# Order and queues of the first transfers, the products ahead of the data, and the place of one q fetch, in a linear-attention and gated-MLP kernel

## The chip, the cores and the metric

The kernel runs on one core of one Trainium2 chip. The metric is device microseconds of one execution. A core has five engines with instruction queues of their own: PE (TensorE, matrix products), DVE (VectorE), ACT (ScalarE), POOL (GpSimd) and SP (SyncE, which here only issues transfers). Each engine works its instructions off in program order and waits where an operand is not ready. Sixteen DMA engines move the data; transfers are issued from SP, ACT or POOL.

## The reference

The inputs are q, k and v with shape (8, 8, 576, 64): batches, heads, tokens and head size, in fp32. The weights w_in (512 x 2048) and w_out (2048 x 512) come in 64-bit floating point.

```python
kv  = einsum('bhsd,bhse->bhde', k, v)          # 64 x 64 per head
o   = einsum('bhsd,bhde->bhse', q, kv)
rms = sqrt(mean(o * o, axis=-1) + 1e-6)
x   = (o / rms * g_norm)                       # heads side by side: (4608, 512)
h   = x @ w_in
sp  = maximum(h, 0) + log1p(exp(-abs(h)))      # softplus
out = (h * erf(sp)) @ w_out                    # (4608, 512)
```

## The kernel before

**Tiling.** The 4608 tokens are worked off in nine groups of 512 (G): T = 0 to 7 are the first 512 tokens of each batch, T = 8 the last 64 tokens of all eight batches together. In a group the heads go in four pairs (p = 0 to 3), since two heads of 64 fill the 128 partitions. After attention a group has xT, four blocks of 128 x 512. The hidden layer goes in 16 parts of 128 columns (f = 0 to 15): four products of 128x512 for h, softplus and erf on ACT, the gate h * erf(sp) on DVE, and four products into the output sums, which are made LAG = 5 parts later.

**Groups.** Groups 0 and 1 use plain fp32 products. In the page, one plain fp32 product of 128x512 is two records of L971 or L674. From group 2 on, weights and activations are cut into parts of a shorter format (L618). The 64-bit weights are turned into fp32 while group 0 runs: a raw piece is loaded (load_w, L243), split into exponent and mantissa words on ACT (w_split, L267: L274 and L275) and joined with integer operations on DVE (w_join, L278: L285 to L298). There are RAW = 4 buffers for raw pieces, so a later load waits for a join. The order of pieces is w_order (L301): the parts f = 0 to 3 of w_in alone, then f = 4 and 5 together, two parts of w_out, and so on.

**The front.** Nothing can overlap ahead of group 0, so its attention is written out by hand in ORDER (L61 to L68). Every name there is a small function; name and pair make one step. For a pair p of group 0: kv (the products of k and v, L724), kv_out (DVE copies the two 64x64 blocks, L735), q (four transposes on PE, L741), q_out (ACT copies the result, L745), result (one product, L748), square (ACT, L751), mean (one product with a constant matrix, L755), log, root and again (ACT, L759, L762, L765), and norm_a, norm_b and norm_c (DVE, L768, L773, L780), after which xT of the pair is there. split is one w_split. join is join_load (L823): one w_join, the next raw load and two of the transfers kept in the list to_fetch. tail stands for the 64 last tokens. next0 and next1 call load_pair for pairs 4 and 5, which are the first two pairs of group 1 ("the fifth pair" is pair 4).

**Transfers.** load_pair (L138) issues k, v and q of one pair of group 0: 288 KB, 288 KB and 256 KB. The queues alternate: `sides` is ACT, SP, ACT, ... for pairs 0 and 2 and begins with SP for pair 1; pair 3 is SP alone. So k0, q0, v1, k2 and q2 go from ACT, and v0, k1, q1, v2, k3, v3 and q3 from SP. For group 1 and later, k and v of a pair are issued at once or put in to_fetch, and load_q (L180) puts eight transfers for q into to_fetch, 32 rows with runs of 128 bytes each, because this q is transposed later on DVE in 32x32 blocks (turn, L349, at L353). fetch_some(n) (L198) issues the next n of to_fetch on SP. In group 0 it runs in each join (two), and at the end of each part n (four, L1024). POOL issues the four transfers of q_last and two of g_col.

**Ahead of the data.** DVE fills mean_f and eps_col and casts mean_f to mean_w (L214 to L218). Then PE runs WARM = 24 products of mean_w with itself, 128x128 each (L828 to L830), whose result nobody reads. After them come the first four raw loads (RAW, L831), then ORDER.

**After the front.** The loop over n (L918) runs the 16 parts of group 0 and of group 1. For n = 0, 1 and 2 the products are interleaved by block of xT (L964 to L967); from n = 3 on a part has its four products in a row. At the start of part n = 4 come the products for the kv of pair 4 (prepare, L388) and on DVE kv_kept and turn(1, 0) (keep_prepared, L397); after that part comes the first product of pair 4 with its transposed q (visit, L426, at L433).

Of the kernel before, what the change touches and what calls it, by code (L numbers as in the profile page):

```python
# [39 lines left out]
FP32 = mybir.dt.float32  # L40
FP32R = mybir.dt.float32r
I32 = mybir.dt.int32
# [14 lines left out]
WHOLE = 2  # L57
SHIFT = 4096.0
SQ = 32
WARM = 24  # L60
ORDER = """  # L61
kv0 q0 q_out0 kv_out0 result0 kv1 q1 square0 mean0 kv_out1 q_out1 log0 result1
kv2 kv_out2 root0 square1 q2 again0 q_out2 mean1 norm_a0 tail norm_b0 log1 tail_out
kv3 q3 root1 again1 q_out3 split norm_c0 kv_out3 tail_result result2 result3 square2 split mean2
next0 square3 norm_a1 split mean3 log2 root2 norm_b1 tail_kept again2
join log3 root3 join next1 again3 softplus norm_c1 join norm_a2 split norm_b2 norm_c2 norm_a3
norm_b3 norm_c3 split join
"""  # L68


# [1 line left out]
def kernel(  # L72
# [10 lines left out]
    nc = tc.nc  # L83
    P = 128
# [3 lines left out]
    G = J * P  # L88
# [18 lines left out]
    early = early_room.enter_context(tc.tile_pool(name="early", bufs=2))  # L107
# [21 lines left out]
    def chunks(T):  # L129

        return 6 if T == 0 else 5

    def rows_in(T, c):

        rows = S // chunks(T) // 16 * 16
        return rows + (S - chunks(T) * rows if c == 0 else 0)

    def load_pair(i, later=False):  # L138
        T, p = divmod(i, NP)
        if T >= B:  # L140
            return
        pool = early if i in (2, 3) else kvp
        sides = [nc.scalar, nc.sync] * 3 if i < 3 else [nc.sync] * 6
        sides = sides[i % 2 :]
        for name, got, src in (("k", k_sb, k), ("v", v_sb, v)):
            side = sides.pop(0)
            C = chunks(T)
            rows, rest = rows_in(T, 1), rows_in(T, 0) - rows_in(T, 1)
            t = got[T, p] = pool.tile([rows + rest, 2, C, D], FP32, name=f"{name}_sb", tag=name)
            heads = src[T, 2 * p : 2 * p + 2]  # L150
            due_ = [
                partial(
                    side.dma_start,
                    out=t[:rows].rearrange("r h c d -> r h (c d)"),
                    in_=heads[:, : S - rest].rearrange("h (r c) d -> r h (c d)", c=C),
                )
            ]
            if rest:
                due_.append(
                    partial(  # L160
                        side.dma_start,
                        out=t[rows:, :, 0],
                        in_=heads[:, S - rest :].rearrange("h r d -> r h d"),
                    )
                )
            if later:
                to_fetch.extend(due_)
            else:
                for start in due_:
                    start()  # L170
        if T > 0:
            load_q(i)
            return
        t = pool.tile([P, G if pool is early else S], FP32, name="q_sb", tag="q")
        t = q_sb[T, p] = t[:, 0:G].rearrange("p (j h d) -> p j h d", j=J, h=2)
        sides.pop(0).dma_start(
            out=t, in_=q[T, 2 * p : 2 * p + 2, 0:G, :].rearrange("h (p j) d -> p j h d", j=J)
        )

    def load_q(i):  # L180


        T, p = divmod(i, NP)
        t = q_sb[T, p] = kvp.tile([P, S], FP32, name="q_sb", tag="q")
        for n in range(P // SQ):
            h, w = divmod(n, D // SQ)
            to = t[n * SQ : n * SQ + SQ].rearrange("a (j b) -> a j b", b=SQ)
            for head, js in ((1 - h, slice(0, G // 2 // SQ)), (h, slice(G // 2 // SQ, S // SQ))):
                src = q[T, 2 * p + head, :, w * SQ : w * SQ + SQ]
                to_fetch.append(  # L190
                    partial(
                        nc.sync.dma_start,
                        out=to[:, js],
                        in_=src.rearrange("(j a) b -> a j b", a=SQ)[:, js],
                    )
                )

    def fetch_some(n):  # L198
        for due_ in to_fetch[:n]:
            due_()  # L200
        del to_fetch[:n]

    for i in range(NP):
        load_pair(i)
# [6 lines left out]
    eps_col = const.tile([P, 1], FP32, name="eps_col")  # L211
    mean_w = const.tile([P, P], FP32R, name="mean_w")
    mean_f = early.tile([P, 2 * G], I32, name="mean_f", tag="w_e", bufs=2).bitcast(FP32)[:, 0:P]
    nc.vector.memset(mean_f, 0.0)  # L214
    for i in range(2):
        nc.vector.memset(mean_f[i * D : i * D + D, i * D : i * D + D], 1.0 / D)
# [92 lines left out]
    def w_next(what):  # L309
        i = w_at[what]  # L310
        if i < len(w_order):
            w_at[what] = i + 1
            {"load": load_w, "split": w_split, "join": w_join}[what](*w_order[i][1:])
# [87 lines left out]
    def attention(T, p, in_parts=False):  # L401
# [136 lines left out]
        def loads():  # L538
            load_pair(T * NP + p + 2, later=True)
# [283 lines left out]
    def join_load():  # L823
        w_next("join")
        w_next("load")
        fetch_some(2)

    warm = ps_h.tile([P, G], FP32, name="warm_ps", tag="h")  # L828
    for _ in range(WARM):
        nc.tensor.matmul(warm[:, 0:P], lhsT=mean_w, rhs=mean_w, start=True, stop=True)  # L830
    for _ in range(RAW):  # L831
        w_next("load")
    do = {
# [4 lines left out]
        "split": partial(w_next, "split"),  # L838
        "softplus": softplus_table,
        "join": join_load,  # L840
        "next0": partial(load_pair, NP),
        "next1": partial(load_pair, NP + 1),
    }
    for p in range(NP):
        do |= first_group(p)
# [72 lines left out]
    for n in range(FIRST * FC + 1):  # L918
# [39 lines left out]
        elif T < FIRST:  # L958
# [11 lines left out]
            for i, c in blocks:  # L970
                nc.tensor.matmul(  # L971
                    plain[i],
                    lhsT=w_in_sb[:, i % FC, c],
                    rhs=xT[T][:, c, :],
                    start=(c == 0),
                    stop=(c == KC - 1),
# [97 lines left out]
    for m in range(first_batch, batches + 1):  # L1074
# [3 lines left out]
        if T + 1 < NG:  # L1078
            todo = list(attention(T + 1, b, in_parts=last_))
            if b == 0:  # L1080
                side = late_r if T % 2 == FIRST % 2 else late
# [30 lines left out]
        if m < batches:  # L1112

            pool, tag = (acc, "e") if m % 2 else (wide, "b")
# [102 lines left out]
```

## Time and profile before

| what | us |
|---|---|
| median of 3 runs | 911.84 |
| lowest and highest run | 910.84, 913.04 |
| the profiled execution's time | 912.09 |
| its span in the profile | 910.3 |
| warm-up products (L830), start and length | 1.68, 5.38 |
| first products of k and v (L724), start | 6.99 |
| first h product (L971), start | 25.93 |
| first product with q of the fifth pair (L433), start | 45.51 |

The span is the time between the first and the last instruction that the profiler saw; 1.8 us of the profiled execution lie outside it. Rows of the timeline give the start and the length in us, the engine, the line of the kernel, the operation, "written tile <- read tiles", the shape and how often; in brackets stands how long the engine had been idle and what ended the idle time. PE is a row of products and PEld the loads of their weights; SPq, ACTq and POOLq are the times in which an engine issued a transfer.

### The profile page before, as it was taken

The page shows a single profiled execution, that of the slowest core. Times are in us where ns is not written, and L with a number is a line of the kernel's source. Part 1 is how long each engine was busy: PE and PEld are TensorE (multiplying, and loading weights), DVE is VectorE, ACT ScalarE, POOL GpSimd, SP SyncE. Part 2 cuts the span into 40 slices and gives each one's busy share as a digit, 9 for nine tenths or more (in the row PEclk, how much of TensorE's full clock was granted, in tenths as well). Part 3 has the DMA queues.
Part 4 walks back from the last instruction along what each step waited for, and adds up shares of the span by engine and source line. Part 5 has one row for each costly group of instructions (what it writes and reads, how often), then busy time and mean ns, then how long its engine had stood idle before and what let it go on. Part 6 is the DMA issues. An engine that isn't in the chain of part 4 may idle for free.

```text
span 910.3 us, 13631 instructions
## 1 busy us (share of the span) xinstructions
PE 901.2 (99%) x5014; PEld 673.4 (74%) x5014; DVE 749.3 (82%) x1084; ACT 593.5 (65%) x784; POOL 4.7 (1%) x14
## 2 busy tenths in 40 slices
PE   8999999999999999999999999999999999999998
PEld 6344445666678888888888888888888888888886
DVE  2799958997688888888888888888888888887777
ACT  4977666776766667667666666666666666665552
POOL 2000000000000000000000000000000000000000
PEclk9999999999999999999999999999999999999999
DMA  9877507999699998999799989999897787778871
GB/s 273 237 244 220 156 0 259 356 365 357 191 337 357 352 323 274 328 348 328 260 327 349 312 277 306 341 326 310 277 354 266 268 319 302 286 285 319 319 263 49
DMA packets 145506, 259.91 MB, mean 286 GB/s; under 512 B 81504, under 2 KB 104032, under 8 KB 145440
## 3 DMA queue, kind: packets, MB, share of 16 engines
q1 hardware_dynamic: 142144, 256.98, 82.6%
q10 hardware_dynamic: 3104, 1.93, 0.8%
q8 instruction: 40, 0.66, 0.3%
q14 instruction: 26, 0.21, 0.1%
q0 software_dynamic: 192, 0.13, 0.1%
HBM read 224.40 MB, written 34.60 MB: 285 GB/s over the span
## 4 chain that ended last, share of the span: by engine, by line
PE 94%; DMA 3%; ACT 1%; DVE 1%; issue 0%; SPq 0%; DVEq 0%
PE n_ps L618 48%; PE m_ps L618 24%; PE o_ps L674 10%; PE h_ps L971 5%; PE at_ps L447 2%; PE at_ps L433 2%; DMA w_out_parts<-w_out 1%; DMA v_sb<-in_v_dram 1%; DMA q_sb<-in_q_dram 1%; PE at_ps L485 1%; PE at_ps L486 1%; DMA w_raw<-in_moe_w_in_dram 1%; PE warm_ps L830 1%; PE kv_ps L724 0%; PE o_ps L748 0%
## 5 line engine op out<-in xcount | busy, mean ns | idle before, releaser
L618 PE MATMUL n_ps<-w_out_parts,g_forms 128*128 128x512 f32 x928 | 230.7, 390 | 0.8 <-DMA w_out_parts<-w_out 0.8
L618 PE MATMUL n_ps<-x_forms,w_in_parts 128*128 128x512 f32 x896 | 224.3, 392 | 0.0
L618 PEld LDWEIGHTS n_ps<-w_out_parts,g_forms 128*128 128x128 f32 x928 | 172.6, 188 | 36.9 <-DMA w_out_parts<-w_out 1.6
L618 PEld LDWEIGHTS n_ps<-x_forms,w_in_parts 128*128 128x128 f32 x896 | 166.6, 188 | 35.7 <-ACT s_sb L916 0.2
L596 DVE TENSOR_TENSOR h<-m_ps,h 128x512 f32<-128x512 f32 x116 | 78.2, 687 | 69.1 <-PE m_ps L618 65.5
L618 PE MATMUL m_ps<-w_out_parts,g_forms 128*128 128x512 f32 (+1 forms) x468 | 124.3, 388 | 0.0
L618 PE MATMUL m_ps<-x_forms,w_in_parts 128*128 128x512 f32 x448 | 119.7, 389 | 0.0
L1123 ACT ACTIVATE h<-n_ps 128x512 f32<-128x512 f32 x112 | 66.2, 594 | 74.0 <-PE n_ps L618 73.7
L1128 ACT ACTIVATE s<-h 128x512 f32<-128x512 f32 x112 | 68.3, 629 | 70.4 <-DVE h L596 70.4
L674 PE MATMUL o_ps<-w_out_sb,h_sb 128*128 128x512 f32 x224 | 101.5, 596 | 0.2 <-DVE h_sb L912 0.2
L618 PEld LDWEIGHTS m_ps<-w_out_parts,g_forms 128*128 128x128 f32 x468 | 87.4, 188 | 18.4
L618 PEld LDWEIGHTS m_ps<-x_forms,w_in_parts 128*128 128x128 f32 x448 | 84.1, 188 | 17.5
L596 DVE TENSOR_TENSOR e<-m_ps,e 128x512 f32<-128x512 f32 (+1 forms) x117 | 80.3, 687 | 15.1 <-PE m_ps L618 5.6
L674 PEld LDWEIGHTS o_ps<-w_out_sb,h_sb 128*128 128x128 f32 x224 | 41.3, 189 | 45.3 <-issue 42.8
L562 DVE SCALAR_TENSOR_TENSOR g_forms<-g_forms 128x1024 fp32r<-128x1024 f32 x58 | 71.1, 1225 | 2.0
L559 DVE TENSOR_TENSOR g_forms<-h,g_forms 128x1024 fp32r<-128x1024 f32 x58 | 70.6, 1217 | 1.2 <-ACT g_forms L556 1.1
L556 ACT ACTIVATE g_forms<-h 128x1024 fp32r<-128x1024 f32 x58 | 58.4, 1049 | 15.2 <-PE m_ps L618 11.1
L591 DVE SCALAR_TENSOR_TENSOR e<-n_ps,e 128x512 f32<-128x512 f32 x88 | 60.2, 684 | 8.1 <-PE n_ps L618 8.1
L1177 DVE TENSOR_TENSOR h<-h,s 128x1024 f32<-128x1024 f32 x56 | 66.0, 1218 | 0.0
L971 PE MATMUL h_ps<-xT,w_in_sb 128*128 128x512 f32 x144 | 65.0, 595 | 0.0
L119 ACT ACT_TABLE_LOAD x44 | 56.5, 1283 | 0.8
L971 PEld LDWEIGHTS h_ps<-xT,w_in_sb 128*128 128x128 f32 x144 | 26.9, 190 | 34.1 <-issue 30.3
(132 smaller groups left out, 1001.7 us busy)
## 6 DMA issues: line engine op xcount, KB each, us to landing
w_out_parts<-w_out SPq DMA_DIRECT2D x116, 768.0 KB, 7.5
w_in_parts<-w_in SPq DMA_DIRECT2D x112, 768.0 KB, 6.9
w_in<-w_new SPq DMA_DIRECT2D x16, 768.0 KB, 4.7
w_raw<-in_moe_w_in_dram SPq DMA_DIRECT2D x16, 512.0 KB, 5.3
w_raw<-in_moe_w_out_dram SPq DMA_DIRECT2D x8, 1024.0 KB, 5.3
out_dram<-e SPq DMA_DIRECT2D x32, 256.0 KB, 3.3
k_sb<-in_k_dram SPq DMA_DIRECT2D x28, 280.0 KB, 6.9
v_sb<-in_v_dram SPq DMA_DIRECT2D x28, 280.0 KB, 7.1
```

What stands on the lines that cost most here:

```text
L119: nc.scalar.preload_act_table_set("softplus")
L556: nc.scalar.activation(high, x, AF.Copy, scale=1.0 + 2.0**-13)
L559: nc.vector.tensor_tensor(out=low, in0=x, in1=high.bitcast(FP32), op=ALU.subtract)
L562: nc.vector.scalar_tensor_tensor(out=both, in0=low.bitcast(FP32), scalar=SHIFT, in1=high.bitcast(FP32), op0=ALU.mult, op1=ALU.add,)
L591: nc.vector.scalar_tensor_tensor(out=out_, in0=ps, scalar=scale, in1=out_, op0=ALU.mult, op1=ALU.add)
L596: nc.vector.tensor_tensor(out=out_, in0=ps, in1=out_, op=ALU.add)
L618: nc.tensor.matmul(ps[:, cols], lhsT=weights(form, k), rhs=moving(form, k)[:, cols], start=(form == forms[0] and k == 0), stop=(form == fo ...
L674: nc.tensor.matmul(o_ps[j], lhsT=g[:, j * P : j * P + P], rhs=w_out_sb[:, f, :], start=(f == 0), stop=last,)
L971: nc.tensor.matmul(plain[i], lhsT=w_in_sb[:, i % FC, c], rhs=xT[T][:, c, :], start=(c == 0), stop=(c == KC - 1),)
L1123: nc.scalar.activation(h[:, i], n_ps, AF.Copy, scale=SHIFT - 1.0)
L1128: nc.scalar.activation(s[:, i], h[:, i], AF.Softplus)
L1177: nc.vector.tensor_tensor(out=part(h, half), in0=part(h, half), in1=part(s, half), op=ALU.mult)
```

## The change

The change has four parts.

1. In load_pair all transfers of k, v and q of group 0's pairs go from SP, in the order pair by pair k, v, q. Only v of pair 0 goes from ACT.
2. DVE first fills a tile `ones` of 128 x 512 with 1.0. In place of the 24 products of 128x128, PE runs two plain fp32 products of 128 columns of it with all of it.
3. join no longer issues two transfers of to_fetch. A step of its own, fetch, issues four. It stands in ORDER after next0 and after the first, third and fourth join.
4. WARM goes.

```diff
-WARM = 24
 ORDER = """
 kv0 q0 q_out0 kv_out0 result0 kv1 q1 square0 mean0 kv_out1 q_out1 log0 result1
 kv2 kv_out2 root0 square1 q2 again0 q_out2 mean1 norm_a0 tail norm_b0 log1 tail_out
 kv3 q3 root1 again1 q_out3 split norm_c0 kv_out3 tail_result result2 result3 square2 split mean2
-next0 square3 norm_a1 split mean3 log2 root2 norm_b1 tail_kept again2
-join log3 root3 join next1 again3 softplus norm_c1 join norm_a2 split norm_b2 norm_c2 norm_a3
-norm_b3 norm_c3 split join
+next0 fetch square3 norm_a1 split mean3 log2 root2 norm_b1 tail_kept again2
+join fetch log3 root3 join next1 again3 softplus norm_c1 join fetch norm_a2 split norm_b2 norm_c2 norm_a3
+norm_b3 norm_c3 split join fetch
 """
...
         pool = early if i in (2, 3) else kvp
-        sides = [nc.scalar, nc.sync] * 3 if i < 3 else [nc.sync] * 6
-        sides = sides[i % 2 :]
         for name, got, src in (("k", k_sb, k), ("v", v_sb, v)):
-            side = sides.pop(0)
+            side = nc.scalar if (i, name) == (0, "v") else nc.sync
...
-        sides.pop(0).dma_start(
+        nc.sync.dma_start(
...
+    ones = early.tile([P, G], I32, name="ones", tag="w_m", bufs=2).bitcast(FP32)
+    nc.vector.memset(ones, 1.0)
     nc.vector.memset(mean_f, 0.0)
...
     def join_load():
         w_next("join")
         w_next("load")
-        fetch_some(2)
 
     warm = ps_h.tile([P, G], FP32, name="warm_ps", tag="h")
-    for _ in range(WARM):
-        nc.tensor.matmul(warm[:, 0:P], lhsT=mean_w, rhs=mean_w, start=True, stop=True)
+    for _ in range(2):
+        nc.tensor.matmul(warm, lhsT=ones[:, 0:P], rhs=ones, start=True, stop=True)
...
         "next1": partial(load_pair, NP + 1),
+        "fetch": partial(fetch_some, 4),
```

## The prediction

> **What bounds the kernel now.** I read the page's chain of waits first, then the timeline of the first 50 us, then the bytes moved in stretches of that front, then the waits of PE.
>
> ```profile
> PE 901.2 (99%) x5014; PEld 673.4 (74%) x5014; DVE 749.3 (82%) x1084; ACT 593.5 (65%) x784; POOL 4.7 (1%) x14
> ...
> PE 94%; DMA 3%; ACT 1%; DVE 1%; issue 0%; SPq 0%; DVEq 0%
> ```
>
> PE carries 94% of the chain. From 45.51 us on the chain is PE without a break to 145 us and, but for one transfer near 246 us, to the end. So a saving counts when PE reaches that unbroken stretch earlier, and only the first 45 us can give it. These are the rows that set it, in order of start (start, length, engine, line):
>
> ```profile
> 1.68 5.38 PE L830 MATMUL warm_ps<-mean_w 128*128 128x128 f32 x24 [1.68 <-DVE eps_col L218]
> ...
> 6.99 1.55 PE L724 MATMUL kv_ps<-v_sb,k_sb 96*64 96x64 f32 x24
> ...
> 10.27 2.08 PE L748 MATMUL o_ps<-qT,bd_first 128*128 128x512 f32 x2 [0.68 <-ACT qT L745]
> ...
> 16.02 0.69 ACT L759 ACTIVATE rms_r<-ms_ps,eps_col 128x512 f32<-128x512 f32 x1 [0.53 <-PE ms_ps L755]
> ...
> 16.77 0.92 PE L724 MATMUL kv_ps<-v_sb,k_sb 96*64 96x64 f32 x24
> ...
> 21.09 0.57 ACT L745 COPY qT<-o_ps 128x512 f32<-128x512 f32 x1
> ...
> 24.31 0.60 ACT L751 ACTIVATE qT<-o_ps 128x512 f32<-128x512 f32 x1
> ...
> 25.93 14.41 PE L971 MATMUL h_ps<-xT,w_in_sb 128*128 128x512 f32 x32
> ...
> 44.58 0.78 DVE L353 STREAM_TRANSPOSE qT<-q_sb 128x576 f32<-128x576 f32 x1 [2.65 <-DMA q_sb<-in_q_dram]
> ```
>
> Four things are seen here. The warm-up holds PE from 1.68 to 7.06 us, and kv0 starts at 6.99 with no idle time before it. PE is then at half speed: kv takes 1.55 at 6.99 and at 12.27 but 0.92 at 16.77, and result0 2.08 where later pieces of 128x512 take 0.86. From log0 at 16.02 ACT has hardly a gap until 34.6 us: its order log0, root0, ..., q_out3 (21.09), split, square2, split, square3 (24.31) is what PE's mean3, and behind it the first h product at 25.5 to 25.9, waits for. Last, DVE waits 2.65 us for the q of the fifth pair, and PE with it:
>
> ```profile
> PE at_ps L433 <- DVE qT L353: 0.8, 1, 0.8
> ```
>
> The stretches (start:end, their length, PE, PEld, DVE, ACT, POOL busy, PEclk, DMA share, GB/s):
>
> ```profile
> 2.00:16.00 14.00, 13.32 (x85) 10.43 (x85) 0.89 (x4) 1.77 (x4) 3.33 (x7) 1.00 1.09 287
> 16.00:22.00 6.00, 5.99 (x71) 4.13 (x71) 3.92 (x10) 5.61 (x10) 0.00 (x0) 1.00 1.06 352
> ...
> 42.00:46.50 4.50, 3.70 (x49) 1.79 (x51) 1.88 (x3) 4.46 (x7) 0.00 (x0) 1.00 0.43 65
> ```
>
> The transfers fill 2 to 22 us and then leave two holes, 22 to 25.5 (42 GB/s in the same view) and 42 to 46.5. The granted clock reads 1.00 throughout, so the half speed shows only in durations.
>
> **What the Trainium skill says.** "TensorE: Matmul & The Clock Gate", Part 1: PE runs at half clock until one free-running window of about 3.4 us was busy, and an idle window sends it back. The trace agrees in kind: L724 falls from 1.55 to 0.92. It also shows that 24 small products do not open the gate: each takes 224 ns (5.38 / 24), of which the weight load is 216 (5.19 / 24). "DMA: Bandwidth & Descriptors", section Issuing engines are not separate DMA queues: all queues run on the same 16 DMA engines and interleave, so a second issuer saves only issue time. That fits 287 GB/s with three issuers and 352 with SP alone, though the rows moved differ too. The same page, Why small descriptors are slow, bears on q's 128-byte rows: in 42 to 46.5 us, when little else moved, 65 GB/s at a share of 0.43, some 151 GB/s if full.
>
> **The change, step by step.**
>
> Warm-up. The 24 products (5.38 us) go. Added is a memset of 128x512 on DVE, ahead of the others: 128x128 took 0.17 and 128x256 took 0.27, so 0.47. It ends near 1.3 and PE starts at 1.35 instead of 1.68. A dense fp32 product of 128x512 takes 0.86 at full clock (3.43 for four at L971), so 1.72 at half clock (the 2.08 of result0 is the upper bound), and two take 3.4, to about 4.8 us. The other memsets come 0.47 later and nobody needs them before 8 us.
>
> First data. k0 and v0 landed at 5.4 (0.76 + 4.6) and 4.9 (0.73 + 4.2) while sharing the engines with k1 and q0. Alone in front on two queues they need 590 KB, reached at about 4.0 to 4.3 by the same GB/s, plus about 0.6 from last byte to landing: 4.9. So kv0 starts at 4.9 instead of 6.99: 2.1 us. ACT loses four issues, which lay in its idle time; SP gains four of 0.4 to 0.75, about 1.6 us of issue per pair against 2.9 us of transfer (852 KB at 287), so hidden.
>
> Clock. From kv0 to log0 the trace has 9.03 us (6.99 to 16.02). At full speed the same order is kv0 0.85, q0 0.6, q_out0 0.65, result0 0.9, kv1 0.85, q1 0.6, mean0 0.9: 5.35 us. How soon the gate opens isn't shown. If the two products fill one window it is at once; if the window's phase is bad, it needs kv0 and q0 behind them as well (busy to some 7.5 us). I take the middle, about 6.2, which costs 0.5: log0 at 10.75, 5.3 us sooner. Lower bound: gate as late as now, see below.
>
> Data of the later pairs. log0 to q_out3 took 5.07 with all data there, so ACT alone would give 15.8. q3 is the 3.54th MB (four pairs of 852 KB, q_last 131 KB). At 287 GB/s from 2.2 us it is moved at 14.5 and lands about 0.9 later (q3 landed at 7.96 + 7.7 = 15.7 now): 15.4, then transposes 0.66: q_out3 at 16.1. At 352 GB/s ACT sets it, 15.8. I take 16.1: 5.0 us sooner than 21.09. w_in's second part (4.59th MB) would land near 18.5 at 287 GB/s, and below 17.5 as soon as the weights run at 352 as now; split wants it at 23.19 - 5.0 = 18.2. Square3, mean3 and the first h product then move by 5.0 too.
>
> Fifth pair's q. Four of its eight transfers now stand behind next0, ahead of the load of weights 4 and 5, and four behind the first join. SP issues one in about 0.47 (0.94 for two), 3.8 us in all, moved ahead of w_out0 and k5, v5; POOL is not passed. They delay weights 4 and 5 by 147 KB at 151 GB/s, 1.0 us (2.3 at 65 GB/s). By bytes these weights land at about 27.2 (28.5), and ACT wants them at 32.41 - 5.0 = 27.4: a wait of at most 1.1 us, hidden because the copy of h behind it already idles 0.61 for PE, and PE needs no bank of it back before the sixth product, 5.8 us after the copy's end (40.96 to 46.80). The 0.80 us of PE idle goes. What is late next: DVE must join w_out0 and gate before the first o product; it needs 4.0 us of joins and 0.7, and gets 2.65 back, while PE reaches that product only 0.8 sooner. The q5 transfers come one product earlier into DMA time that is free.
>
> Sum against the profiled execution (span 910.3, its time 912.09, 1.8 outside): -5.0 - 0.8 = -5.8, so **906.3**. The median shown, 911.84, is 0.25 below the profiled one, inside the runs' own spread of 2.2, and I leave that out. Best case, gate at once and ACT the limit: 5.5 + 0.8, plus up to 0.6 if ACT's own gaps close: 905.2. Weak case, gate near 10 us: the first pair runs at half speed, 1.9 more: 908.2.
>
> **Rivals.** First, the clock stays low as long as now, to about 15.4 us. For it: 24 products and kv0 did not open it in 6.9 us. Against: these were bound by weight loads, and the new ones are dense. Then kv0 at 4.9 plus 9.03 gives log0 at 13.9, and the next stretch pays some 0.7: 1.4 sooner, with q 2.2: 909.9. Second, the front gains but the first group's stage gives it back: DVE is busy 14.4 of the 15 us from 45 to 60 and from 60 to 75, and the holes in the transfers, some 8 us, are what is compressed. Against it: DVE's share is fed by the same front and moves with it, PE has almost no wait there, and the weight parts land 3 to 6 us before their split (w_out's first at 34.3 against 37.51, its second at 43.5 against 49.32). Only the q stall stays: 911.3. Third, slower: one queue alone moves the first data slower than two. The first h product is at the landing of w_in's second part plus 2.3 us (23.19 to 25.5), so break-even, with the 0.8, is a landing at 24.0, or 4.59 MB from 2.2 us at 210 GB/s. At 180 it would be 27.7, h at 30.0, and 912.09 + 4.5 - 0.8 = 915.8. Against it: 352 GB/s on one queue at 16 to 22 us.
>
> **How the numbers follow.** Forecast 906.3: 0.75, with its own range 904.6 to 908.4. Clock late: 0.11. Given back: 0.08. One queue slow: 0.06. A measurement of this kernel tells about 0.2%, 1.8 us, from no change. The forecast is all faster; the late clock at -2.2 is split 0.07 to 0.04; the second rival is no change. So faster 0.82, same 0.12, slower 0.06. The range 904.3 to 909.9 holds the forecast and about half of the late clock, some 0.8.
>
> **What would show it.** The warm row: two products of 1.7 us, ending near 4.8. kv0 near 4.9 and result0 at 0.9 to 1.2, not 2.08. log0 near 10.7, q_out3 near 16, first h product near 20.7. No wait of DVE on q at L353 and none of PE at L433. A bandwidth below 250 GB/s in 2 to 14 us, or DMA waits at split on ACT, would make the prediction wrong, and so would new waits of PE between 40 and 100 us.

## The result and the profile after

Five runs of each kernel beside one another: 907.43 us after (906.94 to 908.57) against 911.26 before (910.84 to 913.04), a ratio of 0.9957, 95% interval 0.9942 to 0.9971. So it is faster by 3.8 us, 0.43%; forecast were 906.3 and 5.8 us. The profiled execution of the changed kernel took 908.57, with a span of 906.8: 3.5 below the span of before.

First the page of the kernel after, its busy times and the shares of its chain of waits by engine:

```profile
PE 897.8 (99%) x4994; PEld 667.9 (74%) x4994; DVE 749.3 (83%) x1085; ACT 593.4 (65%) x784; POOL 4.7 (1%) x14
...
PE 94%; ACT 2%; DMA 2%; DVE 1%; issue 0%; SPq 0%; DVEq 0%; ACTq 0%
```

PE did 3.4 us less and is as full as before: what was taken away is mostly PE's own warm-up and slow products. New in the chain is ACT's second place. Then the timeline of the kernel after, the rows that answer to those of before (lines are one or two lower than there: L723 was L724, L747 was L748, L758 was L759, L970 was L971):

```profile
1.44 3.78 PE L828 MATMUL warm_ps<-ones 128*128 128x512 f32 x4 [1.44 <-DVE ones L212]
...
5.63 0.92 PE L723 MATMUL kv_ps<-v_sb,k_sb 96*64 96x64 f32 x24 [0.41 <-DMA v_sb<-in_v_dram]
...
7.03 0.63 PE L740 MATMUL o_ps<-ident,q_sb 128*128 128x128 f32 x4 [0.48 <-DMA q_sb<-in_q_dram]
...
8.33 1.91 PE L747 MATMUL o_ps<-qT,bd_first 128*128 128x512 f32 x2 [0.67 <-ACT qT L744]
10.18 1.55 PE L723 MATMUL kv_ps<-v_sb,k_sb 96*64 96x64 f32 x24
...
13.33 0.69 ACT L758 ACTIVATE rms_r<-ms_ps,eps_col 128x512 f32<-128x512 f32 x1 [0.28 <-PE ms_ps L754]
...
18.49 0.57 ACT L744 COPY qT<-o_ps 128x512 f32<-128x512 f32 x1
...
23.29 14.43 PE L970 MATMUL h_ps<-xT,w_in_sb 128*128 128x512 f32 x32
...
39.39 0.78 DVE L352 STREAM_TRANSPOSE qT<-q_sb 128x576 f32<-128x576 f32 x1
...
42.02 0.66 PE L432 MATMUL at_ps<-qT,bd_kv 64*64 64x256 f32 x8
```

The reader is to see four things. The two dense products do speed PE up: kv0 takes 0.92 and q0 0.63, where before kv took 1.55. But then result0 takes 1.91 and kv1 1.55: PE is slow again. log0 starts 2.7 us sooner than before (16.02), not 5.3. And the waits on q of the fifth pair are gone: L352 has no bracket.

The trace records when the granted clock of PE changes: it is full from 5.12 us, half from 8.54 and full again from 11.95. These stretches of the kernel after show the same (start:end, length, busy PE, PEld, DVE, ACT, POOL, PEclk, DMA share, GB/s):

```profile
5.12:8.54 3.42, 1.86 (x30) 1.44 (x30) 0.44 (x2) 0.59 (x1) 0.00 (x0) 1.00 1.14 276
8.54:11.95 3.41, 3.41 (x28) 1.79 (x28) 0.17 (x1) 0.60 (x1) 0.22 (x1) 0.50 1.15 272
11.95:15.36 3.41, 3.41 (x35) 1.94 (x34) 0.43 (x3) 2.58 (x5) 0.00 (x0) 1.00 1.15 275
```

PEclk falls to 0.50 for 3.41 us, behind a stretch of the same length in which PE was busy 1.86. In the kernel before the first such record, full speed, comes at 15.25 us. The PEclk of 1.00 that its page shows ahead of that was not recorded, and durations alone tell how slow PE was there.

Last the new wait. This is the chain of waits of the kernel after, where it leaves PE (start, length, what):

```profile
43.82 1.16 ACT w_m L274
...
46.02 0.59 ACT qT L451
46.63 0.22 DVE x_last L454
...
48.98 1.24 DVE w_e L290
50.24 1.24 DVE w_in_sb L297
...
51.52 3.70 PE h_ps L970 x8
```

In the kernel before, the chain was PE's without a break from 45.51 on. Now it runs over ACT (from 37.76), and over DVE's join of the weights' part 6, until 51.52. The saving at the fifth pair's first product is 3.49 us (45.51 to 42.02); at the h product behind that join it is 3.16 (54.68 to 51.52).

### The profile page after: what moved, and what is told of

Its sections match the earlier page's. It is cut to its first block, busy times and chain, and to the rows that moved or that the text cites. A ratio compares the mean times of both kernels' runs of the same rounds, so it can differ in the third digit from the quotient of the medians.

```text
span 906.8 us, 13592 instructions
## 1 busy us (share of the span) xinstructions
PE 897.8 (99%) x4994; PEld 667.9 (74%) x4994; DVE 749.3 (83%) x1085; ACT 593.4 (65%) x784; POOL 4.7 (1%) x14
## 4 chain that ended last, share of the span: by engine, by line
PE 94%; ACT 2%; DMA 2%; DVE 1%; issue 0%; SPq 0%; DVEq 0%; ACTq 0%
PE n_ps L617 48%; PE m_ps L617 24%; PE o_ps L673 10%; PE h_ps L970 6%; PE at_ps L446 2%; PE at_ps L432 2%; DMA w_out_parts<-w_out 1%; PE at_ps L484 1%; PE at_ps L485 1%; DMA q_sb<-in_q_dram 1%; PE ms_ps L754 0%; PE o_ps L747 0%; PE kv_ps L723 0%; PE o_ps L740 0%; DVE h L911 0%
## 5 line engine op out<-in xcount | busy, mean ns | idle before, releaser
L970 PE MATMUL h_ps<-xT,w_in_sb 128*128 128x512 f32 x144 | 65.0, 596 | 0.2 <-DVE w_in_sb L297 0.2
L970 PEld LDWEIGHTS h_ps<-xT,w_in_sb 128*128 128x128 f32 x144 | 26.9, 190 | 34.5 <-issue 30.1
```

The lines of the kernel that those rows point to most:

```text
L970: nc.tensor.matmul(plain[i], lhsT=w_in_sb[:, i % FC, c], rhs=xT[T][:, c, :], start=(c == 0), stop=(c == KC - 1),)
```

## The experiments

Each run stood beside runs of the kernel before in its session: medians 911.71 (43 runs; the first four kernels below), 911.61 (32; the next four), 911.64 (37; the last four). The ratios are to those.

**1 to 4. The parts, alone and together.** The first is the kernel before with `ones` and the two products in place of the 24:

```diff
+    nc.vector.memset(ones, 1.0)
...
-    for _ in range(WARM):
-        nc.tensor.matmul(warm[:, 0:P], lhsT=mean_w, rhs=mean_w, start=True, stop=True)
+    for _ in range(2):
+        nc.tensor.matmul(warm, lhsT=ones[:, 0:P], rhs=ones, start=True, stop=True)
```

> The two dense products alone, queues and fetch as before. Theory A (the front gains from the freed PE and the clock): kv0 starts near 5.5, when k0 lands (5.4 before), log0 near 13.5 to 14.0 instead of 16.02, and the total falls by 2.0 to 2.8 us. Rival B (the queue order is what gains): log0 stays at 15 or later and the total falls by less than 1 us.

The second is the kernel before with the transfers of load_pair from SP:

```diff
-            side = sides.pop(0)
+            side = nc.scalar if (i, name) == (0, "v") else nc.sync
```

> The transfers from SP in order alone, 24 products and fetch as before. Theory A: kv0 stays at 7.0 behind the 24 products and at half speed, log0 near 16.0, total within 0.5 us of before. Rival B: log0 at 14 or earlier, total 2 us or more below.

The third is the kernel before with the fetches as steps of their own:

```diff
-next0 square3 norm_a1 split mean3 log2 root2 norm_b1 tail_kept again2
+next0 fetch square3 norm_a1 split mean3 log2 root2 norm_b1 tail_kept again2
...
-        fetch_some(2)
```

> The fetch steps alone. Theory A: the front is as before up to the first h product (25.9), DVE's wait of 2.65 us on q at the transpose and PE's 0.8 are gone, total down by 0.8 us. Rival (a weight load behind the fetches is late and takes it back): ACT waits before the fifth split, total unchanged.

The fourth has both of these edits, second and third, and the 24 products of before:

> The changed kernel with the 24 small products put back. Theory A: log0 near 16.0 as before, total 0.8 us below before, so 3 us above the changed kernel. Rival B: total 2.5 us or more below before.

Measured: warm-up alone 909.77 (13 runs), ratio 0.9979 [0.9971, 0.9988]; queue alone 911.24 (14), 1.0000 [0.9990, 1.0011]; fetch alone 911.62 (13), 0.9996 [0.9988, 1.0004]; queue and fetch 911.50 (13), 0.9993 [0.9985, 1.0001]. Without the new warm-up nothing can be told from no change, and alone it gives half. The parts don't add: 0.21, 0.00 and 0.04% against 0.43% together. The expected 0.8 us of the fetch came neither in the third nor in the fourth. In the trace of the second, PE:

```profile
6.99 1.55 PE L722 MATMUL kv_ps<-v_sb,k_sb 96*64 96x64 f32 x24
...
10.26 2.07 PE L746 MATMUL o_ps<-qT,bd_first 128*128 128x512 f32 x2 [0.68 <-ACT qT L743]
```

The data comes in the new order, and nobody is there to take it: the 24 products hold PE until 7.06. In the fetch alone PE's first product with the fifth pair's q comes 18.73 us behind the first h product (26.51 to 45.24), as in the kernel after (23.29 to 42.02) and 0.85 less than before (25.93 to 45.51). It is lost again a little later: the h product behind the join of part 6 starts at 54.75, where it was before (54.68), because ACT's square at L452 and behind it DVE's joins are no sooner. The weights of parts 4 and 5 are issued at 24.70 against 24.10, but not because of the fetch: in both executions SP waits at this load until DVE's first join has freed the buffer (24.65 and 24.05).

**5, 6. Keeping PE busy.** The fifth is the kernel after with a product of 128x256 behind kv0 and one behind q0, the sixth the kernel after with a third warm-up product:

```diff
+    fill = {"kv0": 256, "q0": 256}
...
+        n = fill.get(name, 0)
+        if n:
+            nc.tensor.matmul(warm[:, 0:n], lhsT=ones[:, 0:P], rhs=ones[:, 0:n], start=True, stop=True)
```

> The changed kernel with one more product of ones (128x256) behind kv0 and one behind q0, so that PE has work while it waits for q0 and for ACT. Theory A (the gate closed again at 8.3 because PE idled between 6.5 and 8.3): result0 0.9 to 1.0 instead of 1.91, kv1 0.9 instead of 1.55, log0 at 11.7 to 12.0 instead of 13.33, first h product near 22.0 instead of 23.29, total 1.0 to 1.5 us below the changed kernel and its runs no longer in two groups. Rival B (the transfers set the front, q3 landing at 16.2): log0 earlier, but q_out3 not before 18.2 and the total unchanged.

```diff
-    for _ in range(2):
+    for _ in range(3):
         nc.tensor.matmul(warm, lhsT=ones[:, 0:P], rhs=ones, start=True, stop=True)
```

> The changed kernel with three dense products in place of two. kv0 starts near 6.1 instead of 5.63, q0 near 7.0 as now, since it waits for its data. Theory A: the idle time in front of q0 goes, that in front of result0 (0.67) stays; the gate closes in fewer of the runs or later, total between 0 and 1.2 us below the changed kernel. Rival B: total unchanged or up by 0.1 to 0.5 us.

Measured: 907.70 (5 runs), ratio 0.9950 [0.9936, 0.9963], and 907.61 (5), 0.9954 [0.9941, 0.9966]. In both traces PE stays fast. In the fifth log0 comes at 12.25, q_out3 at 17.81 and the first h product only at 23.07; PE waits there for q of pair 2 (0.21) and v of pair 3 (0.32), and the total can't be told from that of the kernel after. That is nearer to rival B than to theory A. The timeline with three products:

```profile
8.24 1.12 PE L747 MATMUL o_ps<-qT,bd_first 128*128 128x512 f32 x2 [0.68 <-ACT qT L744]
...
29.96 1.16 ACT L273 ACTIVATE w_e<-w_raw 128x1024 f32<-128x1024 f32 x1 [1.33 <-DMA w_raw<-in_moe_w_in_dram]
...
50.23 3.70 PE L970 MATMUL h_ps<-xT,w_in_sb 128*128 128x512 f32 x8 [0.54 <-DVE w_in_sb L297]
```

result0 is at full speed, log0 starts at 11.70 and the first h product at 21.67, 1.6 us sooner than in the profile after. Yet the split of parts 4 and 5 starts at 29.96, where it was in the kernel after (29.99): ACT now waits 1.33 us for the weights. (In the ninth and twelfth the profile puts this wait down to DVE's joins of the part before, L290 or L297. But the later of the two transfers lands at 29.85, 29.90 and 31.36 in the sixth, ninth and twelfth, and each split begins 0.10 to 0.11 us behind that: the weights' landing is what it waits for.) So a faster front is held up at these weights, and the span is 905.6, 1.2 below that of the kernel after.

**7, 8. Does q_last take the first data's bandwidth?** q_last's four transfers move from POOL to SP, behind the issues of pair 2 (the two tiny transfers of g_col so come sooner on POOL); the eighth is the fifth with this too.

```diff
+        if i == 2:
+            for p in range(NP):
+                nc.sync.dma_start(
...
-    for p in range(NP):
-        nc.gpsimd.dma_start(
```

> The changed kernel with the four q_last transfers (131 KB in rows of 256 bytes) issued from SP behind pair 2 instead of from POOL at the start. If they take bandwidth from the first data: kv0 at 5.1 to 5.3 instead of 5.63 and q0 at 6.4 to 6.6 instead of 7.03; total 0.3 to 0.6 us below the changed kernel. If not: kv0 unchanged, and q3 and the weights at the same time as now.

> Products as bridge and q_last late together. Theory A: log0 at 11.2 to 11.6, q_out3 then set by the landing of q3 near 16.2 (16.9), first h product near 21.6, total 1.5 to 2.0 us below the changed kernel. Rival B: total within 0.4 us of the changed kernel.

Measured: 910.00 (12 runs), ratio 0.9980 [0.9972, 0.9988], and 910.23 (21), 0.9984 [0.9977, 0.9991]: the eighth 2.5 us slower than the fifth of the same session, from which it differs by this alone. The idea falls. kv0 starts at 5.46 as ever, q0 only at 8.19. SP's row of the seventh shows one cause of the loss:

```profile
8.07 3.94 SPq L204 DMA_DIRECT2D q_last<-in_q_dram  x4
```

Four transfers of 32 KB held SP for 3.94 us, and k of pair 3 was issued at 12.05 (6.99 in the kernel after). Why q0 landed over a microsecond later is open; in 4 to 6 us only 195 GB/s moved, against 296 in the kernel after.

**9 to 12. The kernel after once more, and how much warm-up.** The ninth is the kernel after, unchanged:

> The changed kernel once more, beside the next three on one chip. Theory A2 (the gate closes again in some executions and costs 1.3 us there, the transfers bind in the others): runs in two groups, about 907.0 to 907.4 with a mean clock of 0.999 or 1.000 and 908.2 to 908.8 with 0.998. If the groups are chance: one spread, without order by clock.

The tenth is the kernel after with two transfers in each join as before, and no fetch steps:

```diff
-next0 fetch square3 norm_a1 split mean3 log2 root2 norm_b1 tail_kept again2
+next0 square3 norm_a1 split mean3 log2 root2 norm_b1 tail_kept again2
...
+        fetch_some(2)
```

> The changed kernel with the fetches where they were. Theory A2: the first h product as in the changed kernel, DVE waits on q at its transpose again, PE's wait before the first product with q 0.2 to 1.0; total 0.3 to 0.9 us above the changed kernel. If the fetch steps cost what they gain (their issue holds up the weights): no difference.

The eleventh has one warm-up product, the twelfth two and one of 128x256:

```diff
-    for _ in range(2):
+    for _ in range(1):
```

> The changed kernel with one dense product in place of two, ending near 3.2. The first products run at half speed in all executions and PE idles more. If the gate is what the two products are for: kv0 1.5, result0 1.9 to 2.1, kv1 1.5, log0 at 14.0 to 15.0 and the total 0.8 to 2.0 us above the changed kernel. If only the freed time counts (PE free before the data): no difference to the changed kernel.

```diff
+    nc.tensor.matmul(warm[:, 0 : 2 * P], lhsT=ones[:, 0:P], rhs=ones[:, 0 : 2 * P], start=True, stop=True)
```

> The changed kernel with a third product of half the width, so that PE is busy until kv0's data without delaying kv0 by more than 0.1 us. Theory A2: the gate stays open as with three products, kv0 near 5.7 instead of 6.07, but q2, v3 and the raw weights now bind: total 906.8 to 907.6, no run above 908.2. If the transfers did not bind: 906.3 or below.

Measured: the kernel after again 908.28 (6 runs, 906.87 to 909.69), ratio 0.9965 [0.9953, 0.9977]; no fetch steps 909.84 (21), 0.9980 [0.9973, 0.9986]; one product 909.64 (15), 0.9979 [0.9972, 0.9987]; two and a half 907.00 (5), 0.9954 [0.9942, 0.9966].

The ninth tells most, because its profiled execution (907.89, span 906.1) is of the same kernel and kept its speed. PE in it:

```profile
7.84 1.12 PE L747 MATMUL o_ps<-qT,bd_first 128*128 128x512 f32 x2 [0.68 <-ACT qT L744]
8.89 0.92 PE L723 MATMUL kv_ps<-v_sb,k_sb 96*64 96x64 f32 x24
...
21.68 14.04 PE L970 MATMUL h_ps<-xT,w_in_sb 128*128 128x512 f32 x32
...
40.02 0.66 PE L432 MATMUL at_ps<-qT,bd_kv 64*64 64x256 f32 x8
...
50.25 3.70 PE L970 MATMUL h_ps<-xT,w_in_sb 128*128 128x512 f32 x8 [0.94 <-DVE w_in_sb L297]
```

So whether result0 takes 1.91 or 1.12 changes from one execution to the next. That the longer executions of the set would be those with a mean clock of 0.998 did not come true: none has less than 0.999, the shortest, 906.87, has that, and 909.69 has 1.000.

What holds the front up, on SP in the same execution (then SP's waits: line, waited for, us in total, times, longest):

```profile
17.60 6.07 SPq L197 DMA_DIRECT2D q_sb<-in_q_dram  x4
24.03 0.94 SPq L247 DMA_DIRECT2D w_raw<-in_moe_w_in_dram  x2
```

```profile
SPq L197 <- DMA w_raw<-in_moe_w_in_dram: 4.7, 3, 2.7
```

And on DVE the join that frees the buffer which the weights' load writes, and two rows further on:

```profile
18.73 0.69 DVE L290 SCALAR_TENSOR_TENSOR w_e<-w_raw,w_e 128x512 int32<-128x512 int32 x1
...
45.37 0.22 DVE L454 COPY x_last<-at_ps 128x64 f32<-128x64 f32 x1 [2.70 <-ACT qT L451]
...
48.97 1.23 DVE L297 CUSTOM_DVE_ANT_0 w_in_sb<-w_e,w_m 128x2048 uint16<-128x2048 uint16 x1
```

The buffer is free at 19.42. But four small transfers of q, ahead of the load on SP, hold SP from 17.60 to 23.67, 4.7 us of it waiting for earlier weight transfers to end, and the load goes out at 24.03. Meanwhile the stretches show the DMA engines first full and then about half busy, with a quarter of the bytes:

```profile
20.00:22.00 2.00, 1.50 (x4) 0.68 (x4) 1.83 (x4) 1.25 (x3) 0.00 (x0) 1.00 1.10 319
22.00:24.00 2.00, 2.00 (x6) 0.93 (x5) 1.84 (x4) 1.94 (x5) 0.00 (x0) 1.00 0.41 81
24.00:26.00 2.00, 2.00 (x6) 0.80 (x6) 1.96 (x3) 1.94 (x4) 0.00 (x0) 1.00 0.52 83
```

What SP waits for stands in the trace's records of the instructions. The transfers from SP and ACT have eight completion semaphores, used in turn, and from the ninth transfer on each is held until the one eight places earlier has landed. In the ninth experiment the second, third and fourth of these q transfers begin at 18.27, 21.34 and 23.36, within 0.02 us of the landing of the second, third and fourth load of the first weights (18.25, 21.33, 23.35). The load of parts 4 and 5 follows k of pair 4, which landed at 23.96. Without the fetch ahead of it the same load is issued 0.05 us after its buffer comes free, at 22.09 (first experiment) and 22.88 (tenth), in fronts that are not faster. In the eleventh one product of 2.08 us is not enough: PE is slow from kv0 (1.55) to kv1 (1.55), log0 comes at 14.53, and the kernel is no better than with the fetch left out.

## Why the prediction was right, and where not

The table puts the prediction's steps beside four profiled executions (start in us).

| | before | predicted | after | after again (9th) | three products (6th) |
|---|---|---|---|---|---|
| end of warm-up | 7.06 | 4.8 | 5.22 | 5.22 | 6.14 |
| kv0 | 6.99 | 4.9 | 5.63 | 5.44 | 6.07 |
| log0 | 16.02 | 10.75 | 13.33 | 11.29 | 11.70 |
| first h product | 25.93 | 20.7 | 23.29 | 21.68 | 21.67 |
| split of parts 4 and 5 | 32.41 | 27.4 | 29.99 | 30.01 | 29.96 |
| first product with q of the fifth pair | 45.51 | 39.7 | 42.02 | 40.02 | 40.40 |
| h product behind the join of part 6 | 54.68 | 48.9 | 51.52 | 50.25 | 50.23 |
| span | 910.3 | 904.5 | 906.8 | 906.1 | 905.6 |

(The last three predicted figures are those of before less 5.8. PE's ends are modelled, so that a row can end some 0.1 us behind the start of the next.)

**Warm-up and First data: right in kind, a little short.** The products took 3.78 for 3.4 (one alone takes 2.08 in the eleventh, not 1.72), and kv0 waited 0.41 (0.22 in the ninth) for v0: 1.36 to 1.55 us gained of 2.1. The 0.6 from last byte to landing has no figure behind it in the prediction; k0 and v0 landed at 5.16 and 5.50 (4.86 and 5.31 in the ninth). That the 24 products, and not the transfers, kept PE from the first data is shown by experiments 2 and 1: with the new queue order and the old warm-up kv0 stays at 6.99, with the new warm-up and the old order it is at 5.36. The Trainium skill, "TensorE: Matmul & The Clock Gate", Part 1, which the prediction drew on, holds in this: dense products bring PE to full speed, and one of 2.08 us does not. But being busy for a window is not enough: PE worked without a pause from 1.68 to 9.6 us in the kernel before and was not at full speed until 15.25.

**Clock: the term of the sum that was mis-sized.** kv0 to log0 was put at 5.85, with the gate open once for all. It is 7.70 in the profile after, and 5.85 in the ninth. The prediction asked only when the gate opens, and not whether it stays open: in the kernel after PE was idle 0.41, 0.48 and 0.67 us between 5.2 and 8.3, waiting for v0, q0 and ACT's copy, and was slow from 8.33 to about 11.7. In the ninth the pauses were 0.22, 0.17 and 0.68, full speed was granted from 5.31 on, and the stretch of the same length was busier:

```profile
5.31:8.72 3.41, 2.43 (x30) 1.53 (x30) 0.44 (x2) 0.59 (x1) 0.00 (x0) 1.00 1.11 271
```

The other traces with the dense products fit. In the 3.41 us after full speed was first granted PE was busy 1.40, 1.68 and 1.96 us in the seventh, first and tenth, which lost it, and 1.96, 2.61, 2.73 and 2.73 in the eighth, fifth, sixth and twelfth, which kept it. With 1.96 on both sides, busy time alone does not draw the line. The same page speaks of a whole idle window of about 3.4 us; the length agrees with the records, but here PE lost its speed behind one that was about half busy. By the page the window also runs free of the kernel. That fits too: full speed was first granted between 4.51 and 6.72 us in these traces, at 5.12 and 5.31 in two executions of one kernel, and the landings differ as well. So one kernel can keep its speed in one execution and lose it in the next; what decides it is argued, not shown.

How much of the runs' times this explains is open. A lost stretch costs half of 3.41 us, 0.19% of 907, and so shows as a mean granted clock of 0.998 or less in a run (an estimate, which fits the profiles: 0.998 after with one, 0.996 in the tenth with two). By that the first experiment lost it in nine of 13 runs, which took 908.94 to 911.51; its three runs with 1.000 took 908.37 to 908.87. The kernel after lost it in two of its five runs, 908.57 and 908.29 against 906.94 to 907.43. But the six runs of the ninth never lost it and still spread from 906.87 to 909.69. A likely reason that the parts don't add is that the warm-up alone, with the old queue order, waits 1.06 us for q0 in its profile (0.48 after) and mostly loses the speed that it won. Experiments 5, 6 and 12, which shorten or fill these pauses, kept full speed in their profiles once they had it; their medians (907.70, 907.61, 907.00) can't be told from 907.43 and 908.28.

**Data of later pairs: right where the clock was.** From log0 to the first h product pass 9.96 us (after), 10.39 (ninth, with 0.40 of PE waiting for v3), 9.97 (sixth); predicted were about 10. The fifth needs 10.82, since there q and v of the later pairs come late. (By the prediction's own 0.9 from moved to landed, w_in's second part would come at 19.1 and not 18.5, later than the 18.2 at which split was to want it. It landed at 18.25 in the ninth, before its split at 18.94.)

**Fifth pair's q: one half right.** The waits of DVE (2.65) and PE (0.80) are gone, and the tenth shows them come back (PE waits 0.7 for L352). But "a wait of at most 1.1 us, hidden because the copy of h behind it already idles 0.61" is the step that failed. The prediction charged the four transfers by their issue (0.47 each) and their bytes (1.0 us). On SP they took 5.66, 6.07 and 5.44 us in the three executions, most of it waiting for weight transfers issued eight places before them, and the load behind them went out at 24.07, 24.03 and 23.30, hardly sooner than before (24.10), though the first h product came 2.6 to 4.3 us sooner. The chain of waits before had shown such waits, between 24.5 and 44 us:

```profile
24.53 5.40 DMA w_raw<-in_moe_w_in_dram
29.94 6.96 DMA v_sb<-in_v_dram
36.92 6.96 DMA q_sb<-in_q_dram
```

The second and the third are issued when the one above has landed, and the third is of the q that DVE waited for. The prediction read the chain only from 45.51 on.

And the cover was not there. From the split of parts 4 and 5 ACT has no gap until the square at L451; DVE's x_last waits for that (2.70 us in the ninth), the join of part 6 is queued behind it, and PE waits for the join. From that split to the h product behind the join the ninth has 20.24 us, the sixth 20.27, the twelfth 20.24 (31.46 to 51.70). So the ninth is 5.49 us ahead at the first product with the fifth pair's q, and 4.43 at the h product; its span ends 4.2 ahead. The second rival, "given back", is true of one microsecond in executions like this one. In the profile after, with the slow clock, it is 0.3.

In sum: forecast -5.8; with the clock kept, -5.49 at the end of the front and -4.2 at the end (ninth); with the clock lost, -3.49 and -3.5 (profile after). The total lies in the range, but the prediction's steps were not all right. The profiled 908.57 is near its weak case, 908.2, by another way: the gate did not open late, it closed again. And two of the signs that it named against itself came: a wait for data at a split of ACT (1.33 us in the sixth, 1.09 in the fifth) and a new wait of PE between 40 and 100 us (0.21 in the profile after, 0.94 in the ninth). The third rival, a slow queue, did not come: 266 GB/s moved from 2 to 4 us and 254 to 296 from 4 to 14.

**Open.** Leaving out the fetch steps costs 1.6 us against the ninth and 2.4 against the five runs after, more than the 0.85 that the traces show. The tenth's profiled execution was slow on PE from 8.37 to 14.6, but its 11 runs with a mean clock of 0.999 or 1.000 have the median of all 21, 909.84, so a lost clock is not the reason. Putting the first fetch behind the first join's load, which should free the issue of the weights, was not tried.

## What to carry to other kernels

A warm-up is worth its time only if it is dense, long enough, and followed by work with few pauses; one that ends before the data lands can lose what it won. A transfer moved ahead of another on a queue can cost the issuing engine's wait for a much earlier transfer, not the issue time that it shows when nothing is outstanding: look up which transfers are still under way at that moment, and which of them it waits for. And a front that gets faster is held by the next load with a fixed place; follow its issue, and the engine without gaps behind it, before adding the gain up to the end.

## What the runs showed of the hardware

- PE's granted clock changed at steps of 3.41 us: full from 5.12, half from 8.54, full from 11.95 (profile after). It was lost behind steps in which PE was busy 1.40 to 1.96 us and kept behind steps with 1.96 to 2.73. A step with 2.96 us of work at half speed did not bring it back in the tenth, one with 3.42 did.
- 24 fp32 products of 128x128, 5.38 us in a row and followed at once by kv0, did not bring PE to full speed; two of 128x512 did, at 5.12 us (profile after).
- A transfer from SP or ACT was held until the one eight places earlier had landed (ninth: issued at 18.27, 21.34 and 23.36, landings at 18.25, 21.33 and 23.35). Four transfers of q, 32 or 40 KB each, which take 1.99 us of SP at 25.05 us in the profile after, took 5.66 at 18.13 in the same execution, with weight loads under way.
- k, v and q in 2 to 14 us moved at 254 to 296 GB/s at a DMA share of 0.9 to 1.2, and in 16 to 20 us, when the weights issued from 10.41 on move, 385 at a share of 1.09 (profile after). Between 4 and 14 us most packets were of 256 bytes, between 16 and 20 us of 1024; that this is the reason is not shown.
